# One load in place of two for sixteen chunks of a down projection, and four idle TensorE products in every turn of the loop

## The chip, the core and the metric

The kernel runs on one core of one Trainium2 chip. The metric is the device time of one execution in microseconds; the median of three executions of the kernel before is 264.18 us (264.03 to 264.19). All data is float32.

## What is computed

One decode step of a transformer layer for 8 sequences with one token each: layer norm, attention over the last 1024 positions of a cache (32 query heads, 4 key and value heads of 128), the output projection and a residual; then a second layer norm, a gated feed-forward block and a second residual.

```python
h  = x + attention(layernorm(x) @ wq, k_cache[:, :, -1024:], v_cache[:, :, -1024:]) @ wo
n  = layernorm(h)
h2 = h + (gelu(n @ w_gate) * (n @ w_up)) @ w_down      # x: 8 x 1024, w_down: 3584 x 1024
```

Nearly all of the work is reading weights and cache once: 111 MB.

## The kernel before

The 111 MB are read as fourteen **passes**, in the order of the list `PASSES`: q0 and q1 (query projection), k0, v0, k1, v1 (cache), o0 and o1 (output projection), g1, g0, u1, u0 (gate and up projection), d0 and d1 (down projection), and a small rest of the down projection behind them. The tile `w` has two halves of 64 KB in each of its 128 partitions. Even passes (q0, k0, k1, o0, g1, u1, d0) are loaded into half 0, odd ones into half 1. SyncE issues every load, in order, on one queue: `load(i)` waits until the products of pass i - 2, which used the same half, are done, and then issues. A full pass has rows of 64 KB (8 MB), g1 and u1 have rows of 48 KB. The two down passes are cut: d0, 64 KB a row, comes as two loads of 32 KB rows (L247, L248), d1, 32 KB a row, as one of 24 KB and one of 8 KB rows. The rest follows in four small loads (L261).

TensorE runs a loop of seven **turns** (L170 to L197), one for each pair of passes. A turn consists of 32 products of the even pass (`products(0, c)`, eight chunks c of four products each, stationary operand `st0`, moving operand in half 0), eight transposes (L183, of use in the attention turns alone), 32 products of the odd pass. In the last turn the odd pass has 16 products only, and then the products of the rest follow (L221, L229). Four products of one chunk go to four groups of 32 columns of the array; each float32 product is two instructions in the trace.

The semaphores that TensorE waits for are taken with `take`, which waits for a count and subtracts it. Ahead of the even pass it waits for 17 on `s_in0`: 16 of them are a load's landing, 1 is the news that the stationary operand `st0` has been written by VectorE or GpSimd. Ahead of chunk 4 it waits for 16 on `s_half0`; in the last turn that is the landing of the second half of d0, and in the six turns before it these counts are there from the start (GpSimd adds them, L275). Ahead of the transposes it waits for `s_p`, ahead of the odd pass for 18 on `s_in1`, and ahead of its chunk 3 for `s_half1`.

What writes `st0` differs by turn: the layer norms (L312) for q0 and g1, `queries_in` for k0 and k1, `heads_in` for o0; u1 uses the operand of g1 again and waits only until the sums of g1 have been taken out of PSUM (L431); for d0 the operand is put together by `chunks_in` on GpSimd (L450) after the sums of u0, a multiplication and a transpose on VectorE. When d0 and d1 are done, VectorE, ScalarE and GpSimd add up their results (`d_sum`, `d_ex`, `pre`), VectorE adds the products of the rest (`bank(7)` into `pre`, then `o_fin` in two pieces), and two stores follow.

Of the kernel before, what the change touches and what calls it, by code (L numbers as in the profile page):

```python
# [8 lines left out]
P = 128  # L9
# [7 lines left out]
NQ = 4  # L17
# [3 lines left out]
HALF = 16384  # L21
GAP = 144
CUT = 160

PASSES = ("q0", "q1", "k0", "v0", "k1", "v1", "o0", "o1", "g1", "g0", "u1", "u0", "d0", "d1")
TURNS = 7


UPPER = 12
# [83 lines left out]
def decode_block(nc, out, x, srcs, W):  # L116
# [9 lines left out]
    dve = Engine(nc, vector, "dve")  # L126
    act = Engine(nc, nc.scalar, "act")
    pool = Engine(nc, nc.gpsimd, "pool")
    sp = Engine(nc, nc.sync, "sp")
    s_x, s_half0, s_half1, s_p, s_id = [nc.alloc_semaphore("s_" + n) for n in ("x", "half0", "half1", "p", "id")]  # L130

    s_in = [nc.alloc_semaphore(f"s_in{s}") for s in range(2)]
    s_dn = [nc.alloc_semaphore(f"s_dn{i}") for i in range(len(PARTS) + 2)]
# [7 lines left out]
    ident = sb("ident", [P, P])  # L141
# [5 lines left out]
    def bank(i, n=1):  # L147
        return banks[:, i * N:(i + n) * N]
# [6 lines left out]
    def take(sem, n):  # L155
        nc.tensor.wait_ge(sem, n).then_inc(sem, -n)  # L156

    def products(s, c):
        for j in range(NQ):
            at = block(s, c, j)  # L160
            ins = nc.tensor.matmul(  # L161
                bank(2 * s + c // 4)[32 * j:32 * j + 32, :],
                st[s][:, (c * NQ + j) * 32:(c * NQ + j + 1) * 32], w[:, at:at + N],
                start=(c % 4 == 0), stop=(c % 4 == 3))
        return ins
# [4 lines left out]
    nc.br("turns", engines=on_pe)  # L170
    with nc.body("turns", valid_engines=on_pe):
        closing = nc.tensor.mark_branch_hint_location()
        take(s_in[0], 17)
        for c in range(NC):
            if c == 4:
                take(s_half0, 16)
            ins = products(0, c)
        ins.then_inc(pe.sem, 1)
        take(s_p, 1)
        for h in range(2):  # L180
            for i in range(KC // 2):
                c = h * KC // 2 + i
                ins = nc.tensor.transpose(pp[h][:, i], p_sb[:, c * P:(c + 1) * P], ident)  # L183
            ins.then_inc(pe.sem, 1)
        take(s_in[1], 18)
        for c in range(4):
            if c == 3:
                take(s_half1, 16)
            ins = products(1, c)
        ins.then_inc(pe.sem, 1)  # L190
        nc.regs_alu(turn, turn, 1, op=ALU.add)
        nc.br_lt(turn, TURNS, on_true="upper", on_false="tail", engines=on_pe)
    with nc.body("upper", valid_engines=on_pe):
        for c in range(4, NC):
            ins = products(1, c)
# [22 lines left out]
    for q in range(PAIRED, rows - 1):  # L218
        for j in range(NQ):
            k = place[q - PAIRED] + j * QW  # L220
            ins = pe(lambda e: e.matmul(  # L221
                bank(7)[32 * j:32 * j + 32, 0:QW], at_[:, q, :], w[:, k:k + QW],
                start=(q == PAIRED), stop=(q == rows - 2)), of[q - PAIRED], inc=False)
    t_quads = pe.mark(ins)
    fin = [(4, 0, CUT), (5, CUT, QW - CUT)]
    for i, (b, c0, n) in enumerate(fin):
        tail_at.append(at)
        for j in range(NQ):
            ins = pe(lambda e: e.matmul(  # L229
                bank(b)[32 * j:32 * j + 32, 0:n], at_[:, rows - 1, :], w[:, at:at + n],  # L230
                start=True, stop=True), (s_dn[len(PARTS) + i], 16), inc=False)
            at += n
        t = pe.mark(ins)
# [3 lines left out]
    def load(i):  # L237
        if i >= 2:
            sp.wait(done(PASSES[i - 2]))
        s = i % 2  # L240
        half = w[:, s * HALF:(s + 1) * HALF]
        src = srcs[i]
        n = src.shape[1]
        if PASSES[i][0] == "d":

            m = n * 3 // 4 if s else n // 2
            nc.sync.dma_start(half[:, 0:m], src[:, 0:m]).then_inc(s_in[s], 16)  # L247
            nc.sync.dma_start(half[:, m:n], src[:, m:n]).then_inc((s_half0, s_half1)[s], 16)  # L248
            return
        at = (HALF - n) // 2  # L250
        nc.sync.dma_start(half[:, at:at + n], src).then_inc(s_in[s], 16)
# [7 lines left out]
    for i, sem in enumerate(s_dn):  # L259
        src = srcs[len(PASSES) + i]  # L260
# [3 lines left out]
    t = pool(lambda e: e.memset(ident, 0.0))  # L264
# [4 lines left out]
    t_id = (s_id, 1)  # L269

    t = pool(lambda e: e.memset(p_sb, 0.0))
    pool.wait(t_id)
    nc.gpsimd.wait_ge(*t).then_inc(s_p, 1)

    for sem in (s_half0, s_half1):  # L275
        nc.gpsimd.wait_ge(*t_id).then_inc(sem, 16 * (TURNS - 1))
    own = sb("own", [P, HB])
    t_own = dve(lambda e: e.tensor_reduce(
        out=own, in_=ident.rearrange("p (a b h) -> p b a h", b=HB, h=REP), axis=AX.XY, op=ALU.add), t_id)
# [1 line left out]
    def layernorm_t(src, name, *deps):  # L281
        bn = sb(name + "_bn", [P, 6])
        t = dve(lambda e: e.bn_stats(bn, src), *deps)
        bq = sb(name + "_bq", [32, NQ, 6])
        for g in range(NQ):
            t = dve(lambda e: e.tensor_copy(bq[:, g], bn[32 * g:32 * g + 32]), t)
        mv = sb(name + "_mv", [32, 2])
        t = dve(lambda e: e.bn_aggr(mv, bq), t)
        ve = sb(name + "_ve", [32, 1])
        t_ve = dve(lambda e: e.tensor_scalar(ve, mv[:, 1:2], EPS, None, op0=ALU.add), t)  # L290
        sd = sb(name + "_sd", [32, 1])
        t = act(lambda e: e.activation(sd, ve, AF.Sqrt), t_ve)  # L292
        r0 = sb(name + "_r0", [32, 1])
        t = dve(lambda e: e.reciprocal(r0, sd), t)
        r1 = sb(name + "_r1", [32, 1])
        t = dve(lambda e: e.scalar_tensor_tensor(r1, r0, r0, ve, op0=ALU.mult, op1=ALU.mult), t)
        r2 = sb(name + "_r2", [32, 1])
        t = dve(lambda e: e.tensor_scalar(r2, r1, -0.5, 1.5, op0=ALU.mult, op1=ALU.add), t)
        s_ = sb(name + "_st", [P, 2])
        t = dve(lambda e: e.tensor_copy(s_[0:32, 0:1], mv[:, 0:1]), t)  # L300
        t = dve(lambda e: e.tensor_mul(s_[0:32, 1:2], r0, r2), t)
        for g in range(1, NQ):
            last = dve(lambda e: e.tensor_copy(s_[32 * g:32 * g + 32], s_[0:32]), t)
        xn = sb(name + "_xn", [P, QW])
        t = dve(lambda e: e.tensor_scalar(
            xn, src, s_[:, 0:1], s_[:, 1:2], op0=ALU.subtract, op1=ALU.mult), last)
        xt = sb(name + "_t", [P, NC, 32])
        t = dve(lambda e: e.transpose(xt.rearrange("p c m -> p (c m)"), xn), t)

        to = [a[:, 0:D].rearrange("p (c j m) -> p c j m", c=NC, j=NQ) for a in st]  # L310
        wide = xt.unsqueeze(2).to_broadcast([P, NC, NQ, 32])
        dve(lambda e: e.tensor_copy(to[0], wide), t, inc=False).then_inc(s_in[0], 1)  # L312
        act(lambda e: e.copy(to[1], wide), t, inc=False).then_inc(s_in[1], 2)  # L313

    layernorm_t(x_sb, "ln1", (s_x, 16))
# [4 lines left out]
    for hf in range(2):  # L320
        q_sb = sb(f"q{hf}", [P, N])
        t = dve(lambda e: e.tensor_scalar(q_sb, bank(2 * hf), scale, None, op0=ALU.mult), done(f"q{hf}"))
        t = dve(lambda e: e.scalar_tensor_tensor(
            q_sb, bank(2 * hf + 1), scale, q_sb, op0=ALU.mult, op1=ALU.add), t)
# [4 lines left out]
    def queries_in(hb, *deps):  # L329

        for half in range(2):
            at = half * N
            to = st[0][:, at:at + HB * 136].rearrange("p (b n) -> p b n", b=HB)
            for hf in range(2):
                ins = dve(lambda e: e.tensor_copy(
                    to[:, :, 64 * hf:64 * hf + 64].rearrange("p b (r n) -> p b r n", r=2)[:, :, :, 0:REP],
                    qt[hf][:, :, HB * hb:HB * hb + HB, 0].rearrange("p (r h) b -> p b r h", r=2)),
                    *deps, inc=False)
        ins.then_inc(s_in[0], 1)

    ot = [sb(f"ot{hb}", [P, NQ, HB, REP]) for hb in range(2)]
    share = [sb(f"share{hb}", [P, HB]) for hb in range(2)]
# [1 line left out]
    def heads_in(s, hb, *deps):  # L344

        to = st[s][:, 0:D].rearrange("p (h d x b k) -> p h d x b k", h=4, d=4, x=2, b=B)
        src = ot[hb][:, :, :, 4 * s:4 * s + 4].rearrange("p d b h -> p h d b")
        return dve(lambda e: e.tensor_copy(
            to[:, :, :, :, HB * hb:HB * hb + HB, 0],
            src.unsqueeze(3).to_broadcast([P, 4, NQ, 2, HB])), *deps, inc=False)  # L350

    queries_in(0, t_qt, t_zero)
    for hb in range(2):
        nmax = sb(f"nmax{hb}", [P, 1])
        t = dve(lambda e: e.tensor_reduce(
            out=nmax, in_=bank(0, 2), axis=AX.X, op=ALU.max, negate=True), done(f"k{hb}"))
# [20 lines left out]
                o_sb, o_sum[:, b * DH:(b + 1) * DH], share[hb][:, b:b + 1], o_sb,  # L377
                op0=ALU.mult, op1=ALU.add), t)
        t_ot = dve(lambda e: e.transpose(ot[hb].rearrange("p d b h -> p (d b h)"), o_sb), t)
    heads_in(0, 1, t_ot).then_inc(s_in[0], 1)  # L380
    heads_in(1, 0)
    heads_in(1, 1).then_inc(s_in[1], 2)

# [12 lines left out]
    t = act(lambda e: e.copy(y_sum, bank(0)), done("o0"))  # L396
# [21 lines left out]
    def chunks_in(s, c0, n, *deps):  # L418

        pool.wait(*deps)  # L420
        at = (c0 - (16 if s else 0)) * 64
        return nc.gpsimd.tensor_copy(  # L422
            st[s][:, at:at + n * 64].rearrange("p (c x m) -> p c x m", c=n, x=2),
            at_[:, c0:c0 + n].unsqueeze(2).to_broadcast([P, n, 2, 32]))
# [3 lines left out]
        return act(lambda e: e.activation(ge[k][:nb], hm[k][0][:nb], AF.Gelu_apprx_tanh), t)  # L428

    t_g1 = sums(hm[1][0], "g1")  # L430
    nc.gpsimd.wait_ge(*t_g1).then_inc(s_in[0], 1)  # L431
    t_g1 = gelu(1, t_g1)
    t_g0 = sums(hm[0][0], "g0")
    nc.gpsimd.wait_ge(*t_g0).then_inc(s_in[1], 2)
# [12 lines left out]
    h0 = hm[0][1]  # L447
    t = dve(lambda e: e.tensor_mul(h0, ge[0], h0), t_g0, t_u0)
    t_at = dve(lambda e: e.transpose(at_[:, UPPER:rows].rearrange("p c m -> p (c m)"), h0), t)
    chunks_in(0, UPPER, 16 - UPPER, t_at).then_inc(s_in[0], 1)  # L450
    chunks_in(1, 16, 8).then_inc(s_in[1], 2)


# [130 lines left out]
```

## Time and profile before

| | us |
|---|---|
| median of three executions | 264.18 |
| the profiled execution | 263.77 |
| its span, first to last instruction | 262.5 |
| TensorE matmuls busy | 136.8 (52%) |
| VectorE busy | 35.9 (14%) |
| ScalarE busy | 19.1 (7%) |
| GpSimd busy | 6.8 (3%) |
| packets of SyncE's DMA queue, share of 16 engines' span | 98.4% |

The profiled execution has 1.27 us outside its span and is 0.41 us under the median. In the views, PE is TensorE's matmuls, PEld its weight loads, DVE VectorE, ACT ScalarE, POOL GpSimd, SPq the sequencer of SyncE that issues loads. The views of instructions in order of time merge neighbours of one kind; the bracket at a row's end is the idle time ahead of it and what ended it. The mean TensorE clock that was granted over the span is 0.771 of full speed.

### The profile page before, as it was taken

The numbers are of one execution on the slowest core, as the hardware profiler recorded it, in microseconds if no ns is written. First come the engines' busy times: TensorE is split into PE (matmuls) and PEld (weight loads), VectorE is DVE, ScalarE is ACT, GpSimd is POOL, SyncE is SP. The second block draws the span as 40 slices with busy tenths as digits, with TensorE's granted clock in tenths as the row PEclk, the third lists the DMA queues.
The fourth block names the chain that finished last, engine by engine and source line by source line (L and its number), as shares of the span: only waits on it lengthen the run. The fifth ranks groups of instructions, "written<-read, shape, count | busy, mean of one in ns | idle before, by whom it ended". The sixth has DMA issues, their size and how long they took to land. (4 is left out here: it accounts for less than half of the span.)

```text
span 262.5 us, 2187 instructions
## 1 busy us (share of the span) xinstructions
PE 136.8 (52%) x960; PEld 42.6 (16%) x960; DVE 35.9 (14%) x98; ACT 19.1 (7%) x28; POOL 6.8 (3%) x16
## 2 busy tenths in 40 slices
PE   0005905806826607627708608539277590585954
PEld 0001301201222102122102202112121130121321
DVE  0060110120130210110120100450101004003013
ACT  1030000000020000110000000210401010000000
POOL 2000100000000000000000100000000001001010
PEclk9999975955865965955956965957959598586899
DMA  8998997999899799989979989997999999799996
GB/s 320 484 410 390 479 479 340 459 479 410 390 479 479 340 459 479 420 380 479 479 330 469 479 380 420 479 479 320 479 434 405 439 479 479 320 454 424 439 390 230
DMA packets 3216, 111.31 MB, mean 424 GB/s; under 512 B 496, under 2 KB 784, under 8 KB 1040
## 3 DMA queue, kind: packets, MB, share of 16 engines
q1 hardware_dynamic: 3024, 111.20, 98.4%
q10 hardware_dynamic: 192, 0.11, 0.1%
HBM read 111.18 MB, written 0.13 MB: 424 GB/s over the span
## 5 line engine op out<-in xcount | busy, mean ns | idle before, releaser
L161 PE MATMUL banks<-w,st 128*32 128x512 f32 x864 | 125.3, 743 | 115.7 <-PEq L156 115.7
L161 PEld LDWEIGHTS banks<-w,st 128*32 128x32 f32 x864 | 34.3, 133 | 201.4 <-issue 201.4
L183 PE MATMUL banks<-ident,p 128*128 128x128 f32 x56 | 9.3, 321 | 6.3 <-PEq L156 6.3
L183 PEld LDWEIGHTS banks<-ident,p 128*128 128x128 f32 x56 | 7.4, 164 | 12.3 <-issue 12.3
L358 ACT ACTIVATE p<-banks,nmax 128x1024 f32<-128x1024 f32 x2 | 2.2, 1113 | 73.5 <-DVE nmax L98 73.5
L98 DVE TENSOR_REDUCE nmax<-banks 128x1 f32<-128x1024 f32 x2 | 2.5, 1225 | 33.8 <-PE banks L161 33.8
L98 DVE TENSOR_TENSOR y_sum<-y_sum,banks 128x512 f32<-128x512 f32 (+1 forms) x4 | 2.1, 552 | 33.6 <-PE banks L161 17.8
L98 DVE TENSOR_SCALAR q<-banks 128x512 f32<-128x512 f32 x2 | 1.4, 692 | 31.3 <-PE banks L161 31.3
L98 DVE TENSOR_TENSOR o_sum<-o_sum,banks 128x512 f32<-128x512 f32 x2 | 1.4, 690 | 29.5 <-ACT o_sum L371 29.5
L98 DVE TENSOR_TENSOR d_sum<-d_sum,banks 128x256 f32<-128x256 f32 (+1 forms) x3 | 1.4, 509 | 17.3 <-POOL d_sum L456 12.1
L397 POOL TENSOR_TENSOR y_sum<-y_sum,x_sb 128x256 f32<-128x256 f32 x1 | 0.7, 722 | 115.7 <-ACT y_sum L396 115.7
L422 POOL COPY st<-at 128x768 f32<-128x768 f32 (+2 forms) x3 | 1.8, 609 | 68.4 <-DVE at L98 68.4
L371 ACT COPY o_sum<-banks 128x512 f32<-128x512 f32 x2 | 1.2, 586 | 26.8 <-PE banks L161 26.8
L98 DVE TENSOR_TENSOR u0s<-u0s,banks 128x512 f32<-128x512 f32 x1 | 0.7, 689 | 16.3 <-ACT u0s L412 16.3
L98 DVE TENSOR_TENSOR g0s<-g0s,banks 128x512 f32<-128x512 f32 x1 | 0.7, 689 | 15.8 <-ACT g0s L412 15.8
L292 ACT ACT_TABLE_LOAD x2 | 2.6, 1283 | 1.7 <-POOL ident L264 1.6
L98 DVE TENSOR_TENSOR u1s<-u1s,banks 96x512 f32<-96x512 f32 x1 | 0.7, 683 | 14.0 <-ACT u1s L415 14.0
L221 PE MATMUL banks<-w,at 128*32 128x256 f32 x24 | 1.7, 387 | 1.5 <-DMA w<-weights 1.5
L313 ACT COPY st<-ln_t 128x1024 f32<-128x1024 f32 x2 | 2.1, 1046 | 5.1 <-DVE ln_t L98 5.1
L98 DVE TENSOR_TENSOR g1s<-g1s,banks 96x512 f32<-96x512 f32 x1 | 0.7, 682 | 10.9 <-ACT g1s L415 10.9
L98 DVE SCALAR_TENSOR_TENSOR o<-o_sum,share,o 128x128 f32<-128x128 f32 x6 | 2.1, 352 | 0.2
L412 ACT COPY u0s<-banks 128x512 f32<-128x512 f32 x1 | 0.6, 585 | 18.7 <-PE banks L161 18.7
(64 smaller groups left out, 39.5 us busy)
## 6 DMA issues: line engine op xcount, KB each, us to landing
w<-weights SPq DMA_DIRECT2D x2, 6144.0 KB, 23.5
w<-weights SPq DMA_DIRECT2D x2, 4096.0 KB, 24.5
w<-weights SPq DMA_DIRECT2D x1, 3072.0 KB, 17.0
w<-weights SPq DMA_DIRECT2D x2, 1024.0 KB, 20.1
w<-weights SPq DMA_DIRECT2D x1, 512.0 KB, 21.9
w<-weights SPq DMA_DIRECT2D x1, 320.0 KB, 22.3
w<-weights SPq DMA_DIRECT2D x1, 192.0 KB, 22.3
w<-weights SPq DMA_DIRECT2D x10, 28.9
```

Of the source, the lines that this page charges most:

```text
L98: ins = getattr(self.eng, n.name)(*n.args, **n.kw)
L161: ins = nc.tensor.matmul(bank(2 * s + c // 4)[32 * j:32 * j + 32, :], st[s][:, (c * NQ + j) * 32:(c * NQ + j + 1) * 32], w[:, at:at + N], ...
L183: ins = nc.tensor.transpose(pp[h][:, i], p_sb[:, c * P:(c + 1) * P], ident)
L221: ins = pe(lambda e: e.matmul(bank(7)[32 * j:32 * j + 32, 0:QW], at_[:, q, :], w[:, k:k + QW], start=(q == PAIRED), stop=(q == rows - 2)), ...
L292: t = act(lambda e: e.activation(sd, ve, AF.Sqrt), t_ve)
L313: act(lambda e: e.copy(to[1], wide), t, inc=False).then_inc(s_in[1], 2)
L358: t = act(lambda e: e.activation(p_sb, bank(0, 2), AF.Exp, bias=nmax, accum_out=tot), t)
L371: t = dve(lambda e: e.tensor_add(o_sum, o_sum, bank(3)), act(lambda e: e.copy(o_sum, bank(2)), done(f"v{hb}")))
L397: t = pool(lambda e: e.tensor_add(y_sum[:, 0:QW], y_sum[:, 0:QW], x_sb), t)
L412: t = act(lambda e: e.copy(out[:nb], bank(b)[:nb]), done(name))
L422: return nc.gpsimd.tensor_copy(st[s][:, at:at + n * 64].rearrange("p (c x m) -> p c x m", c=n, x=2), at_[:, c0:c0 + n].unsqueeze(2).to_bro ...
```

## The change

d0 is loaded by one DMA with rows of 64 KB, by the same line as the other full passes, and the wait ahead of chunk 4 is gone with its semaphore. The single count for the operand moves from `s_in0` to a semaphore of its own, `s_op`. At the head of each turn TensorE first waits for `s_op`, then runs four idle products (the identity matrix as stationary operand, the identity repeated four times as 512 moving columns, written to a bank that nothing reads), and then waits for the load.

```diff
+IDLE = 4
-    s_x, s_half0, s_half1, s_p, s_id = [nc.alloc_semaphore("s_" + n) for n in ("x", "half0", "half1", "p", "id")]
+    s_x, s_op, s_half1, s_p, s_id = [nc.alloc_semaphore("s_" + n) for n in ("x", "op", "half1", "p", "id")]
...
+    def idle():
+
+        nc.tensor.matmul(bank(6), ident, ident.unsqueeze(1).to_broadcast([P, NQ, P]), start=True, stop=True)
...
-        take(s_in[0], 17)
+        take(s_op, 1)
+        for _ in range(IDLE):
+            idle()
+        take(s_in[0], 16)
         for c in range(NC):
-            if c == 4:
-                take(s_half0, 16)
             ins = products(0, c)
...
-        if PASSES[i][0] == "d":
-
-            m = n * 3 // 4 if s else n // 2
+        if PASSES[i] == "d1":
+
+            m = n * 3 // 4
             nc.sync.dma_start(half[:, 0:m], src[:, 0:m]).then_inc(s_in[s], 16)
-            nc.sync.dma_start(half[:, m:n], src[:, m:n]).then_inc((s_half0, s_half1)[s], 16)
+            nc.sync.dma_start(half[:, m:n], src[:, m:n]).then_inc(s_half1, 16)
...
-    for sem in (s_half0, s_half1):
-        nc.gpsimd.wait_ge(*t_id).then_inc(sem, 16 * (TURNS - 1))
+    nc.gpsimd.wait_ge(*t_id).then_inc(s_half1, 16 * (TURNS - 1))
...
-        dve(lambda e: e.tensor_copy(to[0], wide), t, inc=False).then_inc(s_in[0], 1)
+        dve(lambda e: e.tensor_copy(to[0], wide), t, inc=False).then_inc(s_op, 1)
...
```

The same replacement of `s_in[0]` by `s_op` stands in `queries_in`, behind `heads_in(0, 1, t_ot)`, behind the sums of g1, and at the second `chunks_in(0, ...)`.

TensorE, the head of one turn before (`banks<-w,st` are products of a pass, `banks<-ident,p` the transposes):

```order
L161 MATMUL banks<-w,st 32x512 [waits s_in0]
L161 MATMUL banks<-w,st 32x512 x15
L161 MATMUL banks<-w,st 32x512 [waits s_half0]
L161 MATMUL banks<-w,st 32x512 x15
L183 MATMUL banks<-ident,p 128x128 [waits s_p]
```

The same place of the kernel after (L161 is now the line of the idle products, L166 that of the products of a pass):

```order
L161 MATMUL banks<-ident 128x512 [waits s_op]
L161 MATMUL banks<-ident 128x512 x3
L166 MATMUL banks<-w,st 32x512 [waits s_in0]
L166 MATMUL banks<-w,st 32x512 x31
L189 MATMUL banks<-ident,p 128x128 [waits s_p]
```

Four products that need no load stand ahead of the wait for the load, and the wait in the middle of the pass is gone.

## Rows read from the trace of the kernel before

**Rows 1.** The page's part on DMA queues: packets, MB, share of 16 engines' span.

```profile
q1 hardware_dynamic: 3024, 111.20, 98.4%
```

**Rows 2.** TensorE in order of time: start us, us, what, count, idle before.

```profile
22.72 8.78 PE L161 MATMUL banks<-w,st 128*32 128x512 f32 x64 [22.72 <-PEq L156]
...
61.40 9.91 PE L161 MATMUL banks<-w,st 128*32 128x512 f32 x64 [10.00 <-PEq L156]
74.44 1.94 PE L183 MATMUL banks<-ident,p 128*128 128x128 f32 x8 [3.14 <-PEq L156]
...
174.94 9.46 PE L161 MATMUL banks<-w,st 128*32 128x512 f32 x64 [7.47 <-PEq L156]
...
192.06 9.43 PE L161 MATMUL banks<-w,st 128*32 128x512 f32 x64 [6.63 <-PEq L156]
206.59 9.00 PE L161 MATMUL banks<-w,st 128*32 128x512 f32 x64 [5.09 <-PEq L156]
...
225.94 9.56 PE L161 MATMUL banks<-w,st 128*32 128x512 f32 x64 [9.33 <-PEq L156]
238.94 10.06 PE L161 MATMUL banks<-w,st 128*32 128x512 f32 x64 [3.45 <-PEq L156]
248.94 1.09 PE L183 MATMUL banks<-ident,p 128*128 128x128 f32 x8
252.66 3.64 PE L161 MATMUL banks<-w,st 128*32 128x512 f32 x32 [2.64 <-PEq L156]
257.56 1.07 PE L221 MATMUL banks<-w,at 128*32 128x256 f32 x16 [1.25 <-DMA w<-weights]
```

**Rows 3.** TensorE's weight loads in order of time: each starts one step of products.

```profile
26.58 0.14 PEld L161 LDWEIGHTS banks<-w,st 128*32 128x32 f32 x4 [0.29 <-issue]
...
67.26 0.14 PEld L161 LDWEIGHTS banks<-w,st 128*32 128x32 f32 x4 [0.54 <-issue]
...
243.18 0.22 PEld L161 LDWEIGHTS banks<-w,st 128*32 128x32 f32 x4 [0.63 <-issue]
244.03 0.22 PEld L161 LDWEIGHTS banks<-w,st 128*32 128x32 f32 x4 [0.63 <-issue]
245.33 0.19 PEld L161 LDWEIGHTS banks<-w,st 128*32 128x32 f32 x8 [1.07 <-issue]
245.79 0.15 PEld L161 LDWEIGHTS banks<-w,st 128*32 128x32 f32 x4 [0.27 <-issue]
...
247.94 0.16 PEld L161 LDWEIGHTS banks<-w,st 128*32 128x32 f32 x4 [0.27 <-issue]
```

**Rows 4.** Stretches of d0: us, busy by engine, granted clock, DMA share, GB/s.

```profile
238.90:244.60 5.70, 5.66 (x28) 1.57 (x32) 0.00 (x0) 0.00 (x0) 0.45 (x1) 0.50 0.93 398
244.70:249.00 4.30, 4.30 (x41) 1.19 (x34) 0.00 (x0) 0.00 (x0) 0.00 (x0) 1.00 1.00 429
```

**Rows 5.** VectorE and GpSimd in order of time: last writers of `st0`.

```profile
53.74 0.58 DVE L98 COPY st<-qt 128x64 f32<-128x64 f32 x4
...
174.10 0.69 DVE L98 COPY st<-ln_t 128x1024 f32<-128x1024 f32 x1
...
238.40 0.95 POOL L422 COPY st<-at 128x256 f32<-128x256 f32 x2 [17.62 <-DVE at L98]
```

**Rows 6.** VectorE in order of time, from the end of d1 on.

```profile
256.36 0.75 DVE L98 TENSOR_TENSOR d_sum<-d_sum,banks 128x256 f32<-128x256 f32 x2 [5.19 <-PE banks L161]
257.35 0.43 DVE L98 TENSOR_TENSOR pre<-d_sum,d_ex 128x256 f32<-128x256 f32 x1 [0.24 <-POOL d_ex L390]
259.54 0.42 DVE L98 TENSOR_TENSOR pre<-pre,banks 128x256 f32<-128x256 f32 x1 [1.76 <-PE banks L221]
260.28 0.54 DVE L98 TENSOR_TENSOR o_fin<-pre,banks 128x160 f32<-128x160 f32 x2 [0.32 <-PE banks L229]
```

**Rows 7.** SyncE's queue: issues of the first loads; of u1 and u0.

```profile
0.74 51.05 SPq L251 DMA_DIRECT2D w<-weights  x4
...
184.46 17.42 SPq L251 DMA_DIRECT2D w<-weights  x2
```

More of the change, by code (lines that the diff above doesn't have):

```diff
@@ L338, in queries_in @@
                     *deps, inc=False)
-        ins.then_inc(s_in[0], 1)
+        ins.then_inc(s_op, 1)
     ot = [sb(f"ot{hb}", [P, NQ, HB, REP]) for hb in range(2)]
@@ L379, in decode_block @@
         t_ot = dve(lambda e: e.transpose(ot[hb].rearrange("p d b h -> p (d b h)"), o_sb), t)
-    heads_in(0, 1, t_ot).then_inc(s_in[0], 1)
+    heads_in(0, 1, t_ot).then_inc(s_op, 1)
     heads_in(1, 0)
@@ L430, in decode_block @@
     t_g1 = sums(hm[1][0], "g1")
-    nc.gpsimd.wait_ge(*t_g1).then_inc(s_in[0], 1)
+    nc.gpsimd.wait_ge(*t_g1).then_inc(s_op, 1)
     t_g1 = gelu(1, t_g1)
@@ L449, in decode_block @@
     t_at = dve(lambda e: e.transpose(at_[:, UPPER:rows].rearrange("p c m -> p (c m)"), h0), t)
-    chunks_in(0, UPPER, 16 - UPPER, t_at).then_inc(s_in[0], 1)
+    chunks_in(0, UPPER, 16 - UPPER, t_at).then_inc(s_op, 1)
     chunks_in(1, 16, 8).then_inc(s_in[1], 2)
```

## The prediction

> **What bounds the kernel now.** I read the DMA queues first. The packets of SyncE's queue fill 98.4% of what sixteen DMA engines could do in the span [rows 1], and that queue carries all weights and cache. Then TensorE in order of time: every pass starts after an idle stretch [rows 2], so TensorE waits for loads and not the reverse. The starts tell how loads follow one another: u1 at 206.59, u0 at 225.94, 19.35 us apart, which is what 8 MB take. The last products wait for the last small loads (257.56, released by DMA [rows 2]), and the additions at the end wait for these products (259.54, idle 1.76 on TensorE's L221 [rows 6]). So the end is set by the stream of loads; an edit counts if it shortens the stream, lets it run dry, or makes something after it later than the small loads.
>
> Two passes need another look. g1 (174.94) starts when VectorE has written its operand, 174.10 + 0.69 = 174.79 [rows 5]; its load has been there since about 172.7, because g0's load behind it takes 19.35 and is used at 192.06 [rows 2]. And d0 starts at 238.94, after GpSimd's copies [rows 5], runs four chunks, and stops: a step at 244.03, the next at 245.33 [rows 3]. That is the landing of its second half.
>
> **The clock.** TensorE was granted 0.50 (1.2 GHz) from 238.90 to 244.60 and 1.00 (2.4 GHz) from 244.70 on [rows 4]. A step of four products with 512 columns takes 0.85 us at the lower level (243.18 to 244.03) and 0.43 at the upper (245.79 to 247.94 in five steps) [rows 3]; a pass is 16 steps. A pass that begins at the lower level changes after a while: q0 begins at 22.72, and its first fast step ends at 26.58, so 3.4 us are slow; k0 begins at 61.40 and its first fast step stands at 67.26, so up to 5.9 us are slow [rows 2, 3].
>
> **The load of d0 in one.** Removed: one DMA and half the rows of this load. With halves, u0 to the second half of d0 is 245.33 + 0.03 - 225.94 = 19.42 us (a product starts 0.03 after its weight load) against 19.35 for a load of 64 KB rows [rows 2, 3]. Gain for the stream: 0.07 us, all of it at the end. Bounds: nothing, and 0.15, since each of these differences is good to some hundredths and the halves may cost on both sides.
>
> Lost: the first four chunks can no longer run from 238.94 on, under the transfer. All 16 steps of d0 must follow the landing, at 245.3. At full clock: the second half took 245.36 to 248.94 = 3.58 us for 8 steps, so 16 take 3.58 + 8 x 0.43 = 7.02, and the transposes start at 252.35 instead of 248.94. They take 1.09 [rows 2], so d1 starts at 253.45 instead of 252.66 and finds three of its four chunks landed. Before, from d1's start to the first addition on VectorE there were 256.36 - 252.66 = 3.70 us [rows 2, 6], which holds about 0.3 of waiting for the last chunk; without this 3.4. So the additions start at about 256.9 instead of 256.36, 0.5 later. They need 257.35 + 0.43 - 256.36 = 1.42 us and are then done at 258.3; the next one needs the rest's products at 259.54 [rows 6]. Cover left: 1.2 us. On TensorE itself the rest's first products wait for their load until 257.56, and TensorE comes free just before VectorE starts, at 256.8: cover 0.7. So these 3.4 us of work moved behind the landing cost nothing, if d0 runs at full clock. That is what the idle products have to bring about.
>
> **The idle products.** Four float32 products with 512 columns are 8 instructions; no row shows this form (128 stationary columns). From below: the step of the passes, 0.43 or 0.85 for 512 columns [rows 3]. From above: the transposes, which have 128 stationary columns, take 1.94 / 8 for 128 columns at the slow pace [rows 2], times four 0.97 for 512. I take the step, since the column count is the same: with 3.4 to 5.9 us at the lower level (4.0 to 6.9 steps of 0.85, the others at 0.43), 3.4 + 4.0 x 0.43 = 5.1 to 5.9 + 1.1 x 0.43 = 6.4 us; 3.4 if all were at full clock, and 8 x 0.97 = 7.8 at the very most.
>
> *In the last turn* they run from 238.94 until between 244.0 and 245.3, into the landing at 245.3: hidden, and d0 finds the upper level. At 7.8 us they end 1.4 late, which uses up the cover of 1.2 and adds 0.2.
>
> *In the turn of g1* nothing hides them, because the load has landed before the operand. g1 starts at 180.0 to 181.3 instead of 174.94, and at full clock is done 7.0 later. Queued behind it: its sums, g0 (starts at 192.06 by its load, still free), and on SyncE the load of u1, which needs g1's half. It was issued at 184.46 [rows 7], 9.52 after g1's start; now at 187.2 to 188.5. How late may it be? The first load, with nothing ahead of it, was issued at 0.74 [rows 7] and used at 22.72: 21.98, of which 19.35 is transfer, so 2.6 us are needed ahead. g0 lands at 192.06, so the stream runs on if u1 is issued by 189.4. Margin 0.9 to 2.2 us: cost nothing. With 7.8 us it is issued at 189.9: cost 0.5.
>
> *In the other turns* the operand is there first, and the products fall into the wait for the load: for k0, written at 54.3 [rows 5], they end by 60.7 and the load is used at 61.40. Should one of them stick out, the pass gets back some of it by the upper level, and there is room: q0 is done at 22.72 + 8.78 = 31.5 [rows 2], and the next load into its half need be issued only by 22.72 + 19.35 - 2.6 = 39.5.
>
> **Sum.** -0.07 for the load, 0 for d0's later products, 0 for g1: the profiled execution of 263.77 would become 263.7. It is 0.41 under the median of the runs, so the median goes from 264.18 to 264.1. What can be told from no change is about 0.2%, 0.53 us: this is **no change**.
>
> **Rivals.**
>
> *The stream runs dry before u1 (slower).* If products with an identity don't lift the clock, they take 6.8 to 7.8 us in the turn of g1, and g1 is as slow as before: done 174.94 + 6.8 to 7.8 + 9.52 = 191.3 to 192.3, while the load had to be issued by 189.4. That puts 1.9 to 2.9 us of hole into the stream: 266.0 to 267.0. For it: the eight transposes from 74.44 stay at the slow pace throughout (1.94 against 1.09 [rows 2]). Against: that is only 1.94 us of work, and the passes, whose products stream as many columns, rose within 5.9 us. It decides where u1 is issued after 189.4, and is seen as slower beyond 189.9. Chance 0.05.
>
> *d0 at the lower level (slower).* If the clock is low when the load lands, or the idle products end too early to hold it, d0 begins slow for up to 5.9 us and loses half of that, 2.95. Then the additions start at 259.85, `pre` is ready at 261.3 instead of 259.54 less its wait, and `o_fin` starts at 261.7 instead of 260.28: 1.45 later, 265.6. It counts once the loss is over the 1.2 of cover. Against: the gap between the idle products and the landing is at most 1.3 us by the figures above; d1 came after a gap of 2.64 us and was fast, and the shortest gaps with slow work behind them are 3.14 and 3.45 us [rows 2]. Chance 0.06.
>
> *Each load pays its start (faster).* If the second half of d0 paid the 2.6 us that the first load of the kernel pays, one load fewer would save them: 261.6. The 19.42 against 19.35 speak against it: a load that is issued behind a running one pays next to nothing. The Trainium skill, page "DMA: Bandwidth & Descriptors", section "Anatomy of one DMA — SWDGE (gpsimd) path", gives about 2.0 us fixed for each DMA of GpSimd's path, which taken over here would give 262.2, and its section "Rules for kernel authors" says to merge small transfers. The loads here are 4 MB and come from SyncE; the trace shows 0.07, and the measured number decides. Chance 0.02.
>
> **How the numbers follow.** The forecast, nothing within 0.2%, has what is left, 0.87, of which I give 0.02 to faster and 0.02 to slower by terms that are mis-sized (more bytes in a given time; 7.8 us for the idle products in both places, which gives +0.5). Faster 0.02 + 0.02 = 0.04; slower 0.05 + 0.06 + 0.02 = 0.13; same 0.83. The range goes from 263.6, the gain of 0.15 with the spread of 0.16 of the three runs and some for another day, to 264.9, which takes in +0.5 for the longer idle products. The slower rivals at 265.6 and above and the faster one stay outside, 0.13 together.
>
> **What would show it.** Of the kernel after: u0 to d0 19.35 apart with d0 as one merged stretch of some 7 us from 245.3 at clock 1.00; g1 starting 5 to 6.5 us after its operand, and u1 still 14.5 us after g0; the rest's first products released by DMA and not by TensorE's own queue; the additions after d1 starting half a microsecond later, with a wait for L227 still ahead of `pre`. It is wrong if u1 comes later than 14.6 us after g0 (the stream ran dry), if the granted clock in d0 is 0.50, or if the rest's products no longer wait for DMA.

## The result, and the profile after

The kernel after takes 264.49 us in the median of 22 executions (263.71 to 265.61), the kernel before beside it 263.95 us (263.79 to 264.19). The ratio is 1.0023, 95% interval 1.0015 to 1.0031: slower by 0.5 us, just beyond what counts as a change, and the executions of the kernel after lie 1.9 us apart where those of the kernel before lie 0.4 apart. The forecast was no change, 264.1; the median lies inside its range of 263.6 to 264.9, but it moved, and by something that the forecast had put at nothing. A spread that grows nearly fivefold is itself a lead: something in the kernel after goes well in one execution and not in the next.

One execution after, of 264.13 us, was profiled. TensorE in order of time (columns as in [rows 2]; L161 is now the idle products, L166 the products of a pass, L227 the first products of the rest):

```profile
61.86 8.77 PE L166 MATMUL banks<-w,st 128*32 128x512 f32 x64 [3.99 <-PEq L157]
...
174.69 5.72 PE L161 MATMUL banks<-ident 128*128 128x512 f32 x8 [7.47 <-PEq L157]
180.35 7.07 PE L166 MATMUL banks<-w,st 128*32 128x512 f32 x64
...
192.49 8.74 PE L166 MATMUL banks<-w,st 128*32 128x512 f32 x64 [4.05 <-PEq L157]
...
207.03 7.07 PE L166 MATMUL banks<-w,st 128*32 128x512 f32 x64 [2.17 <-PEq L157]
...
226.38 8.86 PE L166 MATMUL banks<-w,st 128*32 128x512 f32 x64 [11.25 <-PEq L157]
238.68 3.67 PE L161 MATMUL banks<-ident 128*128 128x512 f32 x8 [3.45 <-PEq L157]
245.73 7.08 PE L166 MATMUL banks<-w,st 128*32 128x512 f32 x64 [3.37 <-PEq L157]
...
257.94 1.07 PE L227 MATMUL banks<-w,at 128*32 128x256 f32 x16 [0.55 <-DMA w<-weights]
```

SyncE's issues of u1 (the first of the two) and u0, as in [rows 7]:

```profile
187.48 14.13 SPq L257 DMA_DIRECT2D w<-weights  x2
```

VectorE from the end of d1 on, as in [rows 6]:

```profile
257.46 0.75 DVE L99 TENSOR_TENSOR d_sum<-d_sum,banks 128x256 f32<-128x256 f32 x2 [2.49 <-PE banks L166]
258.45 0.42 DVE L99 TENSOR_TENSOR pre<-d_sum,d_ex 128x256 f32<-128x256 f32 x1 [0.24 <-POOL d_ex L395]
...
259.92 0.42 DVE L99 TENSOR_TENSOR pre<-pre,banks 128x256 f32<-128x256 f32 x1 [1.05 <-PE banks L227]
```

In this execution nearly all goes as forecast. u0 to d0 is 245.73 - 226.38 = 19.35, 0.07 less than before. d0 runs in 7.08 us. The rest's products still wait for DMA (0.55), and the next addition still waits 1.05 us for them. g1 starts at 180.35 and u1's load is issued at 187.48, 5.01 us ahead of g0's first product; u1 follows g0 by 207.03 - 192.49 = 14.54, so the stream did not stop. The 0.36 us by which it is longer than the profiled execution before were there already at k0 (61.86 against 61.40 [rows 2]), before anything that the change could reach by way of g1 or d0. So what costs the median half a microsecond is not to be seen in this execution.

A second profiled execution of the same kernel (a1, below) took 264.36 us and shows it:

```profile
175.67 6.39 PE L161 MATMUL banks<-ident 128*128 128x512 f32 x8 [7.47 <-PEq L157]
181.99 7.08 PE L166 MATMUL banks<-w,st 128*32 128x512 f32 x64
...
192.15 7.08 PE L166 MATMUL banks<-w,st 128*32 128x512 f32 x64 [2.06 <-PEq L157]
...
207.28 9.32 PE L166 MATMUL banks<-w,st 128*32 128x512 f32 x64 [4.42 <-PEq L157]
...
239.96 6.67 PE L161 MATMUL banks<-ident 128*128 128x512 f32 x8 [3.44 <-PEq L157]
246.56 7.07 PE L166 MATMUL banks<-w,st 128*32 128x512 f32 x64
...
258.17 1.07 PE L227 MATMUL banks<-w,at 128*32 128x256 f32 x16
```

Its load of u1:

```profile
189.12 10.48 SPq L257 DMA_DIRECT2D w<-weights  x2
```

The idle products took 6.39 instead of 5.72 us, g1 was done later, u1's load was issued at 189.12, only 3.03 us ahead of g0's first product, and u1 followed g0 by 207.28 - 192.15 = 15.13: 0.6 us were lost in the stream. That is one of the signs by which the prediction called itself wrong (u1 more than 14.6 us after g0). Of the 1.64 us by which the issue came later than in the first execution, 0.98 are the start of the idle products (175.67 against 174.69): g1's operand is made from o1's result, and o1 took 9.94 us here against 8.61; its granted clock was 0.50 until about 164 here, until about 162 there.

### The profile page after: what moved, and what is told of

Same layout as the page of the kernel before. It is cut to its first block, busy times and chain, and to the rows that moved or that the text cites. A ratio compares the mean times of both kernels' runs of the same rounds, so it can differ in the third digit from the quotient of the medians.

```text
span 262.8 us, 2297 instructions
## 1 busy us (share of the span) xinstructions
PE 149.9 (57%) x1016; PEld 51.1 (19%) x1016; DVE 35.9 (14%) x98; ACT 19.1 (7%) x28; POOL 6.8 (3%) x16
## 5 line engine op out<-in xcount | busy, mean ns | idle before, releaser
L166 PE MATMUL banks<-w,st 128*32 128x512 f32 x864 | 110.2, 667 | 67.4 <-PEq L157 67.4
L166 PEld LDWEIGHTS banks<-w,st 128*32 128x32 f32 x864 | 32.1, 121 | 140.3 <-issue 140.3
L161 PE MATMUL banks<-ident 128*128 128x512 f32 x56 | 29.4, 673 | 36.3 <-PEq L157 36.3
L161 PEld LDWEIGHTS banks<-ident 128*128 128x128 f32 x56 | 11.5, 217 | 53.7 <-issue 53.7
L189 PE MATMUL banks<-ident,p 128*128 128x128 f32 x56 | 8.5, 300 | 6.3 <-PEq L157 6.3
L189 PEld LDWEIGHTS banks<-ident,p 128*128 128x128 f32 x56 | 6.7, 152 | 12.3 <-issue 12.3
L227 PE MATMUL banks<-w,at 128*32 128x256 f32 x24 | 1.7, 387 | 0.8 <-DMA w<-weights 0.8
```

The source lines that it names most:

```text
L161: nc.tensor.matmul(bank(6), ident, ident.unsqueeze(1).to_broadcast([P, NQ, P]), start=True, stop=True)
L166: ins = nc.tensor.matmul(bank(2 * s + c // 4)[32 * j:32 * j + 32, :], st[s][:, (c * NQ + j) * 32:(c * NQ + j + 1) * 32], w[:, at:at + N], ...
L227: ins = pe(lambda e: e.matmul(bank(7)[32 * j:32 * j + 32, 0:QW], at_[:, q, :], w[:, k:k + QW], start=(q == PAIRED), stop=(q == rows - 2)), ...
```

## The experiments

**First round: where is the loss?** Theory A is the end: if the clock is still up after u0, the idle products are short (3.67 us in the rows after), end more than 3 us ahead of the landing, and the clock could fall under d0. Theory B is the turn of g1: its idle products make the load of u1 late.

*e1_no_idle* leaves the idle products out and keeps the one load.

```diff
-IDLE = 4
+IDLE = 0
```

> The kernel after without the four idle products; the load of d0 stays one. Theory A (the clock when d0 lands): with the idle products the clock is up in some executions and down in others when d0 lands; without them TensorE rests for about 10 us before d0, so d0 begins at the lower level in every execution, for 3.4 to 5.9 us, and loses 1.7 to 3.0 us, of which about 1.2 are covered: 264.4 to 265.8, median about 265.1, and d0 one stretch of 8.7 to 10 us from 245.3. Theory B (the idle products in the turn of g1 make the load of u1 late and the stream runs dry): 263.9 as before, since nothing delays g1 any more; u1 14.5 us after g0.

Measured: 264.72 us (264.35 to 265.74), ratio 1.0037 (1.0021 to 1.0053). The profiled execution, of 265.43 us, shows d0 starting at the landing at the lower level (granted clock 0.50 from 245.40 to 251.00), with nothing behind it waiting for DMA any more:

```profile
245.41 9.85 PE L166 MATMUL banks<-w,st 128*32 128x512 f32 x64 [10.06 <-PEq L157]
255.19 1.09 PE L189 MATMUL banks<-ident,p 128*128 128x128 f32 x8
256.21 3.64 PE L166 MATMUL banks<-w,st 128*32 128x512 f32 x32
259.67 1.48 PE L227 MATMUL banks<-w,at 128*32 128x256 f32 x24
```

9.85 against 7.08 is 2.8 us more. Of these 1.5 reach the end in this execution (265.43 against 263.91, the median of before beside it); the cover takes the rest. The median of the seven executions loses 0.8. The stream lost nothing: u1 came 206.70 - 192.17 = 14.53 us after g0. So the end is worth holding the clock for, as theory A says, and the prediction's second rival had its price about right (1.45 us for 2.95 us of loss). The run doesn't say that this happens in the kernel after.

*e2_halves_idle* takes the kernel after and brings d0 back to two loads.

```diff
...
         for c in range(NC):
+            if c == 4:
+                take(s_half0, 16)
             ins = products(0, c)
...
-        if PASSES[i] == "d1":
+        if PASSES[i][0] == "d":
...
```

> The idle products as in the kernel after, but d0 in two loads with the wait ahead of chunk 4, as in the kernel before. Theory A (the clock when d0 lands): 263.9 to 264.0 with a spread of at most 0.5 us, as before, because the first four chunks run under the transfer and leave only eight steps behind the landing. Theory B (the idle products themselves cost, in the turn of g1 or elsewhere): 264.5 with a spread of nearly 2 us, as after.

Measured: 264.15 us (263.83 to 266.36), ratio 1.0015 (1.0000 to 1.0031). The spread is back, with d0 in halves: theory A doesn't explain that. In the profiled execution, of 264.53 us, u1's load was issued at 188.38, and u1 followed g0 by 207.25 - 192.21 = 15.04 us:

```profile
188.38 11.28 SPq L259 DMA_DIRECT2D w<-weights  x2
```

```profile
192.21 7.07 PE L166 MATMUL banks<-w,st 128*32 128x512 f32 x64 [2.86 <-PEq L157]
...
207.25 8.77 PE L166 MATMUL banks<-w,st 128*32 128x512 f32 x64 [4.34 <-PEq L157]
```

*e4_last_four* takes the kernel after and runs the idle products in the last turn alone.

```diff
         take(s_op, 1)
+        nc.br_lt(turn, TURNS - 1, on_true="even", on_false="idles", engines=on_pe)
+    with nc.body("idles", valid_engines=on_pe):
         for _ in range(IDLE):
             idle()
+        nc.tensor.br("even")
+    with nc.body("even", valid_engines=on_pe):
         take(s_in[0], 16)
```

> d0 in one load, and the four idle products in the last turn alone, by a branch on the turn. Theory A (the clock when d0 lands): as after, about 264.5 with executions from 263.7 to 265.6. Theory B (the turn of g1): 263.9 with a spread of at most 0.5 us; g1 starts at 174.9 as before and u1's load is issued at 184.5.

Measured: 263.98 us (263.79 to 264.27), ratio 1.0001 (0.9992 to 1.0009). Theory A falls as the cause: the whole end of the kernel after is in here, and costs nothing. Its mechanism can even be seen, in the slowest execution of the eleven (264.27), which is the profiled one:

```profile
237.96 5.39 PE L161 MATMUL banks<-ident 128*128 128x512 f32 x8 [3.62 <-PEq L157]
245.33 8.77 PE L166 MATMUL banks<-w,st 128*32 128x512 f32 x64 [1.98 <-PEq L157]
254.03 1.09 PE L193 MATMUL banks<-ident,p 128*128 128x128 f32 x8
255.05 3.64 PE L166 MATMUL banks<-w,st 128*32 128x512 f32 x32
258.51 1.48 PE L231 MATMUL banks<-w,at 128*32 128x256 f32 x24
```

Its granted clock in stretches around d0 (columns as in [rows 4]):

```profile
243.40:245.30 1.90, 0.00 (x0) 0.00 (x1) 0.00 (x0) 0.00 (x0) 0.00 (x0) 1.00 0.73 310
245.40:249.00 3.60, 3.60 (x20) 1.17 (x24) 0.00 (x0) 0.00 (x0) 0.00 (x0) 0.54 1.02 437
```

The clock fell about when d0 began, after a rest of 1.98 us, and d0 took 8.77 us; the cover absorbed most of it. In the profiled kernel after, d0 came after a longer rest, 3.37 us, and was fast: the length of the rest alone does not decide.

*a1* is the kernel after once more, with no edit.

> The kernel after once more, for a second profiled execution. Theory A (the clock when d0 lands): its time follows the clock in d0: about 264 if all 16 steps of d0 run in 7.1 us, later by half of what d0 spends at the lower level, less about 1 us of cover. Theory B (the stream runs dry): its time follows the distance from g0 to u1, 14.5 us if the stream ran on, more if not.

Measured: 264.36 us, with the rows above: all 16 steps of d0 in 7.07 us, and u1 15.13 us after g0. One execution does not settle it, but it is what theory B says.

**Second round: is it the late load?** Theory C is B made precise: the loss comes from u1's load being issued late, whatever makes it late. Theory D: the idle products themselves cost a little in every turn.

*e5_only_g1* has d0 in two loads, as before, and idle products in the turn of g1 alone.

```diff
         take(s_op, 1)
+        nc.br_lt(turn, 4, on_true="even", on_false="from_g1", engines=on_pe)
+    with nc.body("from_g1", valid_engines=on_pe):
+        nc.br_lt(turn, 5, on_true="idles", on_false="even", engines=on_pe)
+    with nc.body("idles", valid_engines=on_pe):
         for _ in range(IDLE):
             idle()
...
```

> d0 in two loads as before; the four idle products in the turn of g1 alone, by a branch on the turn. Theory C (the load of u1, issued some 4 us later than before, makes the stream lose time): 264.1 to 264.6 with a spread of over 1 us, u1 15.0 us or more after g0 where the load was issued after 188, 14.5 where it was issued by 187.5. Theory D (idle products cost a little in every turn, by what they read or by the clock): 263.9 to 264.0, u1 14.5 after g0.

Measured: 264.20 us (263.77 to 265.71), ratio 1.0018 (1.0004 to 1.0032). One turn alone brings the loss and the spread. The profiled execution took 264.78 us:

```profile
188.53 11.19 SPq L265 DMA_DIRECT2D w<-weights  x2
```

```profile
175.52 5.94 PE L161 MATMUL banks<-ident 128*128 128x512 f32 x8 [7.79 <-PEq L157]
...
192.26 7.07 PE L166 MATMUL banks<-w,st 128*32 128x512 f32 x64 [2.77 <-PEq L157]
207.57 8.65 PE L166 MATMUL banks<-w,st 128*32 128x512 f32 x64 [8.23 <-PEq L157]
```

*e6_not_g1* is the kernel after with idle products in all turns but that of g1 (the two branch targets of the turn of g1 and of the turns ahead of it are exchanged).

```diff
...
+        nc.br_lt(turn, 4, on_true="idles", on_false="from_g1", engines=on_pe)
+    with nc.body("from_g1", valid_engines=on_pe):
+        nc.br_lt(turn, 5, on_true="even", on_false="idles", engines=on_pe)
...
```

> The kernel after, but without idle products in the turn of g1. Theory C (late load of u1): 263.9 with a spread of about 0.5 us, u1 14.5 us after g0, its load issued at 184.5. Theory D (idle products cost in every turn): 264.4.

Measured: 263.80 us (263.63 to 263.88) beside 263.86 of before, ratio 0.9996 (0.9987 to 1.0005), and the smallest spread of all kernels here. Theory D falls. In its profile:

```profile
192.21 9.41 PE L166 MATMUL banks<-w,st 128*32 128x512 f32 x64 [6.35 <-PEq L157]
...
206.74 7.07 PE L166 MATMUL banks<-w,st 128*32 128x512 f32 x64 [1.49 <-PEq L157]
...
257.64 1.07 PE L233 MATMUL banks<-w,at 128*32 128x256 f32 x16 [0.31 <-DMA w<-weights]
```

u1 is 14.53 us after g0, its load issued at 184.90, and the end waits for DMA. This is the change as the forecast saw it: no cost, and 0.06 us under before, which is too little to tell from nothing.

*e7_only_g1_eight* is e5 with `IDLE = 8`.

> d0 in two loads as before; eight idle products in the turn of g1 alone, none elsewhere. They take 8.5 to 9.9 us, g1 starts at 183.4 to 184.7 and u1's load is issued at 190.6 to 191.9. If 2.6 us ahead of g0's use are enough (the figure of the prediction), the stream loses 1.2 to 2.5 us: 265.1 to 266.4. If the load must be issued more than 4 us ahead (Theory C), it loses 2.7 to 4: 266.6 to 267.9. Theory D: 264.0, since a late load costs nothing.

Measured: 266.36 us (four executions, 265.45 to 267.51), ratio 1.0109 (1.0081 to 1.0136): the loss is there, and its size spans both expectations. The profiled one, of 265.46 us, issued u1's load at 190.28:

```profile
174.31 8.91 PE L161 MATMUL banks<-ident 128*128 128x512 f32 x16 [7.78 <-PEq L157]
...
192.00 7.07 PE L166 MATMUL banks<-w,st 128*32 128x512 f32 x64 [0.75 <-PEq L157]
208.29 8.92 PE L166 MATMUL banks<-w,st 128*32 128x512 f32 x64 [9.22 <-PEq L157]
```

u1 is 16.29 us after g0, 1.76 more than before.

*e8_late_issue* has no idle product at all. It is the kernel before with u1's load held back until ScalarE has run two spare activations.

```diff
...
+        if PASSES[i] == "u1":
+            nc.sync.wait_ge(s_late, 1)
...
-    t_g1 = gelu(1, t_g1)
+    t_sum = t_g1
+    for i in range(2):
+        spare = sb(f"spare{i}", [P, N])
+        act(lambda e: e.activation(spare[:96], hm[1][0][:96], AF.Gelu_apprx_tanh), t_sum)
+    t_g1 = gelu(1, t_sum)
+    nc.scalar.wait_ge(*t_g1).then_inc(s_late, 1)
```

> The kernel before without any idle product; SyncE holds back the load of u1 until ScalarE has run two spare activations and the one that it runs anyway after g1, so that it is issued at about 188.9 instead of 184.5. Theory C (late load of u1): u1 15.0 to 15.2 us after g0 and 264.4 to 264.6. Theory D (the idle products themselves): u1 14.5 after g0 and 263.9.

Measured: 264.45 us (263.76 to 265.52), ratio 1.0022 (1.0009 to 1.0035): the loss and the spread of the kernel after, without its edits. The profiled execution (264.19) was one of the better ones: issued at 189.67, u1 14.68 us after g0.

```profile
189.67 12.89 SPq L254 DMA_DIRECT2D w<-weights  x2
```

```profile
192.31 9.86 PE L162 MATMUL banks<-w,st 128*32 128x512 f32 x64 [5.99 <-PEq L157]
206.99 9.35 PE L162 MATMUL banks<-w,st 128*32 128x512 f32 x64 [4.82 <-PEq L157]
```

**Third round: how late is late?** The same hold, released at other points.

*e10_issue_186* lets the load go when VectorE has the sums of g1.

```diff
...
+    nc.gpsimd.wait_ge(*t_g1).then_inc(s_late, 1)
...
     t_g1 = gelu(1, t_sum)
```

> The kernel before, no idle product; SyncE holds back the load of u1 until VectorE has the sums of g1, so that it is issued at about 186.5, some 5.5 us ahead of g0's use. Theory C, with the point at which it begins to cost between 187.5 and 188.4 as the profiles so far have it: nothing, 263.9, spread as before. If every delay costs something: 264.1.

Measured: 263.95 us (263.77 to 264.08), ratio 1.0002 (0.9993 to 1.0012).

*e9_issue_188* is e8 with `range(0)`, *e11_issue_190* with `range(4)`.

> The same, held back until ScalarE's activation after g1 is done: issued at 187.7 to 188.4, some 4 us ahead of g0's use. Theory C: at the edge, 263.9 to 264.2, single executions up to 0.5 us over the others. By the 2.6 us of the prediction: nothing, 263.9.

Measured: 263.89 us, but from 263.81 to 265.87: seven executions up to 263.94, and three at 264.47, 264.60 and 265.87; ratio 1.0011 (0.9995 to 1.0028). This is the edge.

> The same, with four spare activations ahead: issued at 190.2 to 191, 1 to 1.8 us ahead of g0's use. Theory C: 1.3 to 2.5 us, 265.2 to 266.4, as with eight idle products in the turn of g1. By the 2.6 us of the prediction: 0.8 to 1.6 us, 264.7 to 265.5.

Measured: 265.25 us (264.22 to 265.49), ratio 1.0047 (1.0034 to 1.0060), where the two expectations meet, so the median doesn't tell them apart; e2, e5 and e9 do. So does the profiled execution, of 265.01 us: its load was issued 2.28 us ahead of g0's use, by the 2.6 us it would have lost 0.3, and u1 is 15.72 after g0, 1.19 more than before:

```profile
192.11 9.40 PE L162 MATMUL banks<-w,st 128*32 128x512 f32 x64 [6.67 <-PEq L157]
207.83 8.38 PE L162 MATMUL banks<-w,st 128*32 128x512 f32 x64 [6.31 <-PEq L157]
...
227.18 8.94 PE L162 MATMUL banks<-w,st 128*32 128x512 f32 x64 [9.95 <-PEq L157]
```

What the stream moved when u1's packets took over from g0's, in the kernel before:

```profile
191.00:195.00 4.00, 2.94 (x16) 0.91 (x20) 0.00 (x0) 0.00 (x0) 0.00 (x0) 0.50 1.14 492
```

and in e11:

```profile
191.00:195.00 4.00, 2.89 (x16) 0.91 (x20) 0.00 (x0) 0.00 (x0) 0.00 (x0) 0.50 0.98 369
```

The last column is GB/s: 492 against 369 in these four microseconds (packets count where they start). The column ahead of it is the time that these packets hold the DMA engines, 1.14 against 0.98 of the stretch: it fell by less than the bytes, so the packets were slower. The time is lost at the start of u1's load; u0 follows u1 at the usual 227.18 - 207.83 = 19.35.

The single packets in the traces show where. A packet of u1 is one row of 48 KB, each of the sixteen DMA engines moves eight of them, and in the kernel before every one takes 1.81 or 1.82 us and starts as the packet ahead of it ends. In the executions that lost time the first packets of u1 are longer, up to 3.27 us in e11; the later ones take 1.81 us again, but for a few. In e5 one engine also stood idle for about a microsecond ahead of its first packet, and in e7 at least half of them waited for theirs. The last engine is through its first packet 0.24 (e8), 0.56 (e2), 0.75 (a1), 0.93 (e5), 1.32 (e11) and 1.84 us (e7) later than in the kernel before, counted from the end of g0's last packet; u1 came 0.15, 0.51, 0.60, 0.78, 1.19 and 1.76 us later. That accounts for the whole loss.

All profiled executions, by how far ahead of g0's first product u1's load was issued:

| kernel | issue of u1 | ahead of g0's use, us | longest first packet of u1, us | g0 to u1, us | time of that execution |
|---|---|---|---|---|---|
| e1 (slow d0) | 184.26 | 7.91 | 1.82 | 14.53 | 265.43 |
| before | 184.46 | 7.60 | 1.82 | 14.53 | 263.77 |
| e6 | 184.90 | 7.31 | 1.82 | 14.53 | 263.85 |
| e4 (slow d0) | 185.46 | 6.63 | 1.82 | 14.53 | 264.27 |
| e10 | 186.03 | 6.09 | 1.82 | 14.53 | 263.82 |
| e9 | 187.09 | 5.14 | 1.82 | 14.54 | 263.94 |
| after | 187.48 | 5.01 | 1.82 | 14.54 | 264.13 |
| e2 | 188.38 | 3.83 | 2.68 | 15.04 | 264.53 |
| e5 | 188.53 | 3.73 | 2.71 | 15.31 | 264.78 |
| a1 | 189.12 | 3.03 | 2.48 | 15.13 | 264.36 |
| e8 | 189.67 | 2.64 | 2.33 | 14.68 | 264.19 |
| e11 | 189.83 | 2.28 | 3.27 | 15.72 | 265.01 |
| e7 | 190.28 | 1.72 | 2.95 | 16.29 | 265.46 |

In these thirteen executions nothing is lost with 5 us and more; below 4 us something always is, from 0.15 to 1.8 us. The two latest issues lose most, but the loss does not simply follow the lead: e8, with 2.64 us, lost less than e2 with 3.83. The packets suggest where the edge lies. A row of g0 takes a DMA engine 2.42 us, and the engines begin their last row of g0 from about 188.5 on. The loads without a loss were issued 1.1 us or more ahead of that moment, those with a loss 0.3 us ahead of it or later. This fits all thirteen; no run varied the length of the rows, so it is not shown.

## Why the prediction was wrong

**The step that failed** is "the stream runs on if u1 is issued by 189.4" in the turn of g1, and with it the term "0 for g1" of the sum, which measured about half a microsecond in the median. It took the 2.6 us that the first load needs, with nothing ahead of it, as the lead that a load needs behind a running one. The loads of e2, e5 and a1 were issued at 188.38, 188.53 and 189.12, inside that margin, and lost 0.5, 0.8 and 0.6 us in longer first packets; e5 shows that this turn alone makes the kernel slower, e8 that a load just as late does so without any idle product, and e6 that without it the change is as forecast. The figure needed lies between 3.8 and 5.0 us by the table. The issue was forecast at 187.2 to 188.5. It was 187.48 in one execution and 189.12 in the other, where g1's operand came a microsecond later; the forecast took the operand's time from one execution and left no room for that. So the kernel after lies across the edge: the two profiled executions fall on either side of it. That this is the spread of all 22 is inferred; e8 and e9, which have the spread without the edits, bear it out.

The first rival named the mechanism (the stream suffers before u1), but with a sharp point where it begins, 189.4, and a cause that was wrong: identity products do lift the clock. It was given 0.05. Had the lead been taken as unknown between 2.6 and the 7.60 that the kernel before keeps, this rival would have weighed far more. The evidence for 2.6 was one row from an empty queue, and the forecast rested its "cost nothing" on it without a bound from the other side.

**The stream.** 0.07 us for larger rows: right in the rows, where u0 to d0 is 19.35 after; the times don't resolve it: e6, with idle products everywhere but in the turn of g1, is 0.06 under before, within its interval of no change.

**d0 behind its landing.** 7.02 us were forecast for 16 steps, 7.08 are in the rows. From the restart of d0 to the additions it was 256.36 - 245.36 = 11.00 us before [rows 3, 6] and is 257.46 - 245.73 = 11.73: 0.7 later, not 0.5; the cover was still 1.05 us. e4 and e6 show that it costs nothing.

**The idle products.** 5.1 to 6.4 us were forecast from the lower level; the rows have 5.72, 6.39, 5.94 and, in the last turn of a1, 6.67. There they ended 0.6 us after the load must have landed (226.64 + 19.35 = 245.99, d0 at 246.56). That used up the cover on TensorE: the rest's products start at 258.17 with no wait for DMA, another of the prediction's signs of being wrong. In the last turn of the profiled kernel after they took 3.67, because the clock had not yet fallen. Around them, in columns as in [rows 4]:

```profile
238.70:242.30 3.60, 3.60 (x8) 1.39 (x8) 0.00 (x0) 0.00 (x0) 0.39 (x1) 1.00 1.30 564
242.40:245.70 3.30, 0.00 (x0) 0.01 (x1) 0.00 (x0) 0.00 (x0) 0.00 (x0) 1.00 0.59 251
```

The prediction had full clock as a bound only, and did not draw its consequence: the rest ahead of d0 was 3.37 us, where it allowed at most 1.3. Here the level stayed up through the rest (1.00); e4 shows what can happen instead (8.77 us for d0 after a rest of 1.98), and that this too stays mostly covered.

**The other turns.** They cost nothing, as forecast: e6 has idle products in all of them.

**The second rival** had its place and price about right and did not decide the result; e1 shows that it costs 0.8 us in the median without the idle products. **The third** (each load pays its start) is refuted by the 0.07 that stands in the rows. The start of a load was not free, though: issued in time it is hidden behind the load in front, and issued late it shows as the longer first packets of u1.

## What to carry to other kernels

In a kernel that is bound by its stream of loads, the release of a buffer is a deadline. Ask for each edit on the engine that releases it how late the next load may be issued, and take the lead that the kernel has now as the only one known to suffice, not the start-up time of a first load. When a load loses time, compare the length of its first packets with that of the later ones. Filler work that keeps a clock up belongs where a wait is sure to be long enough for it; one place in a loop where the operand comes last turns filler into delay. And profile more than one execution where the spread has grown, since a single trace may show a good one.

## What the runs showed of the hardware

A load that is issued behind a running one can lose time before the queue is empty: with 3.8 us of the running load left until its use, u1 came 0.5 us late. In a1, e8 and e11 every DMA engine went from g0 to u1 with hardly a break (0.11 us at most), and still the first packets of u1 took up to 2.48, 2.33 and 3.27 us in place of 1.82. The first load of the kernel shows the same with nothing ahead of it: in the kernel before its first packets begin 1.01 us after the issue and take 2.66 to 3.35 us, the later ones 2.42.

The Trainium skill, page "DMA: Bandwidth & Descriptors", section "Specifications", gives some 0.6 us to the first byte for loads issued by SyncE. The traces agree with that figure: the issue takes SyncE 0.33 us, and the first packet starts 0.68 us behind its end for the first load and 0.63 us for u1 in e7, where DMA engines were waiting. By that figure alone none of the other loads would have been late. What makes the first packets of a late load long, and why the loss varies from one execution to the next, was not settled.

Products of an identity with a repeated identity lift the clock too. Around the idle products in the turn of g1 the kernel after was granted:

```profile
174.70:178.80 4.10, 4.10 (x5) 1.81 (x6) 0.00 (x0) 0.26 (x1) 0.00 (x0) 0.50 0.63 272
178.90:187.30 8.40, 8.40 (x68) 2.35 (x66) 0.00 (x0) 0.00 (x0) 0.00 (x0) 1.00 1.15 499
```

They began at 174.69 at the lower level (0.50, 1.2 GHz), the level rose after 4.1 us, still among them, and g1 then ran at the upper one throughout, in 7.07 us where it took 9.46 before [rows 2].
